# A gated linear attention with an MLP mixer on one core: batch 0's attention laid out by token slot, one load queue, and a new order

## The chip, the cores and the metric

The kernel runs on one core of one Trainium2 chip. The metric is device time in microseconds (us) of one execution. A core has five engines with queues of their own: TensorE (PE, matmuls; its weight loads are shown as PEld), VectorE (DVE), ScalarE (ACT), GpSimd (POOL) and SyncE (SP, which only issues transfers). Each queue is worked off in its order; an instruction at its head that waits holds everything behind it.

## The reference

Two parts follow each other. For each of 4 batches and 8 heads, a 48 x 48 state runs over 768 tokens, and its output goes through a mixer over tokens and then over channels:

```python
for t in range(S):                      # S = 768, per batch and head, D = 48
    state = alpha[:, :, t, :, None] * state + einsum('bhd,bhe->bhde', k[:, :, t], v[:, :, t])
    y[:, :, t] = einsum('bhd,bhde->bhe', q[:, :, t], state)
x  = y as (4, 768, 384)
h  = relu(x.T @ w_tok1) @ w_tok2        # 768 -> 256 -> 768, over tokens
u  = x + h.T
h2 = relu(u @ w_ch1) @ w_ch2            # 384 -> 1536 -> 384, over channels
out = u + h2
```

Inputs and output are float32; the kernel multiplies in bf16.

## The kernel before

**Tiling.** The tokens of a batch are cut into three blocks of 256, so there are 12 blocks n = 3b + k. A partition holds two neighbouring tokens, called slots (0 and 1), so 128 partitions hold a block; partitions 0 to 63 are its first half (128 tokens, hf 0), 64 to 127 its second (hf 1). A load (`ld_at`, `ld_kt`, `ld_qt`, `ld_vt`) brings 384 KB.

**Attention of a block.** `ln` takes the logarithm of alpha, a matmul with a triangular matrix (`cum`, `cumw`) sums it up along a half, and two exponentials give E and IE. `qq` = q x E and `kk` = k x IE (L642). Both are transposed: for blocks below NX = 6 on PE (`trk`, `trq`, L654) with a copy out of PSUM (`evk`, `evq`), for later blocks by a DMA transpose on SP (`dk`, `dq`, L664), where q needs one more copy (`pq`). `G0_`, `G1_` multiply keys with queries on quarter tiles of the array (48 rows by 64 columns); `mask` (L700, DVE only) zeroes what lies in the future. `K` sums k v over each half of a block; from it come the states `s0`, `s1`: for a first half directly (L747), else by `sa` (add the earlier state, L750) and `sm` (multiply by the decay, L753). `ia`, `ib` multiply queries with the earlier state and `y0_`, `y1_` add the masked part; `x` (L684 or L685) copies the result out of PSUM. A block yields two x tiles of 128 tokens.

For `K` and `y` to contract over 128 partitions, the tokens of one half have to lie over all partitions: `vs0`, `vs1` swap halves of v, and `ka`, `kb`, `kc` (L722) turn halves of k. These are copies of 64 partitions.

**Batch 0** (blocks 0 to 2, `WIDE`) keeps both slots apart up to the exponentials (`lnw`, `cumw`, L626), and a short `Et` (L630) takes the totals; later blocks fold the slots first (`P`, `k0a`, `q0r`).

**Mixer of a batch.** `t1` (L787) and `ht`, then `t2` (L792) and `u` (L796), then u is transposed: for batches in `UP` = (0, 1) on PE (`up`, L803, with the copies `ut`), for the others by DMA (`ux`, L668). `c1` (L811, 24 groups of three matmuls) and `rt` (L782 on ACT, L784 on DVE), `c2` (L816, groups of three), `o` (L820) and the store `st` (L574). Weights come as float32 in 16 loads (`ldw_`) and are cast (`cw_`). `t2` of batch 0 needs the six x tiles and the casts of w_tok1 and w_tok2.

**The order.** Nothing is scheduled at run time. `ORDER` names every step with its engine in its last letter (t PE, s ACT, v DVE, g POOL, y SP), and each engine's queue is this list with the others left out. `BUFS` names the buffer of each value; 19 buffers of the class `in` hold all loads and raw weights, and a load waits for the last reader of its buffer. Each DMA also waits for an earlier one whose semaphore it takes over. Steps named `f1_...` and `f3_...` are matmuls on a zero tile `zs` whose result is not used; L593 is the helper `mm` through which they and all small matmuls go, so its line stands for many steps. A semaphore also orders DVE and POOL operations that share their SBUF port (`shared`).

Of the kernel before, what the change touches and what calls it, by code (L numbers as in the profile page):

```python
# [11 lines left out]
ALU = mybir.AluOpType  # L12
# [85 lines left out]
NX = 6  # L98
KFN = 0
LAST = (3, 0)  # L100
UP = (0, 1)
# [9 lines left out]
WIDE = (0, 1, 2)  # L111

# [3 lines left out]
def build(g):  # L116
# [8 lines left out]
    def filler(nm, bank):  # L125
        return [P.op(f"f{z}_{nm}", {"PE": pe([512] * z)["PE"], "NONE": (0.0, 0.0)}, -100, writes=[bank],
                     emit=lambda e, z=z: g.fill(bank, z)) for z in (1, 3)]

    def attention(n):
# [8 lines left out]
        def fill(nm, bank):  # L138
            return filler(f"{nm}{n}", bank) if n < NB else []

        at, kt, qt, vt = V("in"), V("in"), V("in"), V("in")
        ld = {}
        for v, nm in ((at, "at"), (kt, "kt"), (qt, "qt"), (vt, "vt")):
            ld[nm] = P.op(f"ld_{nm}{n}", {"SP": (420.0, 420.0), "ACT": (374.0, 374.0)}, -90000.0 + 10 * n, writes=[v],
                          emit=lambda e, v=v, nm=nm: g.load(e, nm, v, b, k, ld[nm]), dma=("i", IN_NS, 1500.0, 650.0))
        la, E, IE = V("la"), V("E"), V("IE")
        pkk, pkq, vb = V("pkk"), V("pkq"), V("vb")
        k_in, q_in = [ld["kt"]], [ld["qt"]]
        if n in WIDE:
            lnp = O("ln", act(800, True), 0, writes=[la], reads=[at], preds=[ld["at"]], emit=lambda e: g.lnw(la, at))  # L150
            cb = V("pair")
            cum = O("cumw", pe([384] * 4 + [4] * 8 + [16]), 2, writes=[cb, E, IE], reads=[la], preds=[lnp] + fill("cumw", cb),
                    emit=lambda e: g.cumw(cb, la))
            e1 = O("E", act(768), 4, writes=[E], reads=[cb], preds=[cum], emit=lambda e: g.exps(E, cb, 1.0))
            et = O("Et", act(16), 6, writes=[E], reads=[cb], preds=[cum], emit=lambda e: g.exptot(E, cb))
            e2 = O("IE", act(768), 3, writes=[IE], reads=[cb], preds=[cum], emit=lambda e: g.exps(IE, cb, -1.0))
        else:
# [8 lines left out]
            e1 = et = O("E", act(400), 4, writes=[E], reads=[cb], preds=[cum], emit=lambda e: g.expE(E, cb))  # L166
            e2 = O("IE", act(384), 4, writes=[IE], reads=[cb], preds=[cum], emit=lambda e: g.expIE(IE, cb))
# [12 lines left out]
        if n < NX:  # L180
            bk, bq = V("one"), V("one")
            trk = O("trk", pe([128] * 8), 8, writes=[bk], reads=[pkk], preds=[kk] + fill("trk", bk),
                    emit=lambda e: g.trw(bk, pkk))
            evk = O("evk", either(dve(1024, True), act(1024)), 9, writes=[tpk], reads=[bk], preds=[trk],
                    emit=lambda e: g.trwev(e, tpk, bk))
            trq = O("trq", pe([128] * 8), 8, writes=[bq], reads=[pkq], preds=[qq] + fill("trq", bq),
                    emit=lambda e: g.trw(bq, pkq))
            evq = O("evq", either(dve(1024 * 1.065), act(1024 * 1.34)), 9, writes=[tpq], reads=[bq], preds=[trq],
                    emit=lambda e: g.qev(e, tpq, g.bank(bq).bitcast(BF16)))
        else:  # L190
            evk = O("dk", {"SP": (1240.0, 1240.0)}, 9, writes=[tpk], reads=[pkk], preds=[kk],
                    emit=lambda e: g.xbar(tpk, pkk), dma=("x", 1400.0, 1180.0, 480.0))
            tqx = V("tpk")
            xq = O("dq", {"SP": (1240.0, 1240.0)}, 9, writes=[tqx], reads=[pkq], preds=[qq],
                   emit=lambda e: g.xbar(tqx, pkq), dma=("x", 1400.0, 1180.0, 480.0))
            evq = O("pq", either(dve(1024), act(1024 * 1.35, True), {"POOL": (1100.0, 1140.0)}), 9.5, port=True, writes=[tpq], reads=[tqx], preds=[xq],
                    emit=lambda e: g.qev(e, tpq, g.t(tqx)))
        gtm = V("gtm")
        masks = []
        for hf in range(2):  # L200
            gp = V("pair")
            G = O(f"G{hf}_", pe([128] * 4), 10 + hf, writes=[gp], reads=[tpk, tpq], preds=[evk, evq] + fill(f"G{hf}", gp),
                  emit=lambda e, hf=hf, gp=gp: g.gmm(gp, tpk, tpq, hf), mode="G")
            masks.append(O(f"mask{hf}_", dve(1024), 12 + hf, writes=[gtm], reads=[gp], preds=[G],
                           emit=lambda e, hf=hf, gp=gp: g.mask(gtm, gp, hf)))
        nst = 2 if k < NB - 1 else 1
        kp = V("pair")
# [4 lines left out]
        vsw = lambda hf, preds: shift(f"vs{hf}_", 10, [vb], [vt], preds, lambda e: g.vswap(e, vb, vt, hf))  # L212
        turned = n >= KFN
        if turned:
            vs = [vsw(hf, [vc]) for hf in range(2)]
            kx, kp_in = None, [kk, vc, vs[0]]
            if nst == 2:
                kx = V("kt")
                ka = shift("ka", 9, [kx], [pkk], [kk], lambda e: g.kturn(e, kx, pkk, 0))
                kb = shift("kb", 9, [kx], [pkk], [kk], lambda e: g.kturn(e, kx, pkk, 1))  # L220
                kp_in += [ka, kb, vs[1]]
            kc = shift("kc", 9, [pkk], [], [kk, trk if n < NX else evk] + ([ka] if nst == 2 else []),
# [4 lines left out]
        else:  # L227
            KO = O("K", {"PE": (276.0 if nst == 2 else 140.0, 420.0)}, 9.5, writes=[kp], reads=[pkk, vb],
                   preds=[kk, vc] + fill("K", kp) + ([prev_s[1]] if prev_s and k > 0 and n > NB else []),
                   emit=lambda e: g.kmm(kp, pkk, vb, nst), mode="G")  # L230
            vs = [vsw(hf, [KO, vc]) for hf in range(2)]
        before = prev_s if k > 0 else None
        states = [before]
        for hf in range(nst):
            s_, sp = V("ss"), states[-1]
            if sp is None:
                so = O(f"s{hf}_", dve(384), 10, writes=[s_], reads=[kp, E], preds=[KO, et],
                       emit=lambda e, s_=s_, hf=hf: g.sfirst(s_, kp, E, hf, wide, turned))
# [636 lines left out]
```

## Time and profile before

| | us |
|---|---|
| runs | 166.53, 166.59, 167.32 (median 166.59) |
| span of the profiled execution, first to last instruction | 165.0 |
| PE busy | 156.2 (1683 matmuls) |
| DVE busy | 121.2 |
| ACT busy | 96.2 |
| POOL busy | 68.7 |
| the 38 matmuls on `zs`, all before 27 us | 12.7 |
| first `t2_0` matmul (L792) | starts at 32.90 |
| first `c1_0` matmul (L811) | starts at 37.34 |
| end of the last `o` (L820) | 162.42 |

The profile gives the profiled execution's span and no other time of it; the median of the runs is 1.6 us above the span. Busy time counts an instruction from start to end. Matmuls overlap, so a matmul of 326 ns can follow another after 162 ns. What an engine waited for is inferred from semaphores. The granted TensorE clock is 1.00 over the whole execution.

Load data come to 25.17 MB read; the DMA engines are busy in 9 tenths or more of nearly every slice up to half of the span.

### The profile page before, as it was taken

What the parts mean: (1) busy time and instruction counts of PE and PEld (TensorE: products, weight loads), DVE (VectorE), ACT (ScalarE), POOL (GpSimd) and SP (SyncE); (2) the same over time, 40 slices, a digit from 0 to 9 for tenths busy, and PEclk for the clock granted to TensorE, in tenths of its full rate; (3) what the DMA queues carried; (4) which work ended last, traced back from release to release, by engine and by line L of the source; (5) the groups of instructions that cost most, each with busy time, mean ns of one, the idle gap of its engine ahead of it and who ended that gap; (6) DMA issues with size and microseconds to landing.
All of it is one profiled execution on the core that took longest, in us unless ns stands there. A gap on an engine that the chain in (4) does not pass through costs nothing.

```text
span 165.0 us, 4235 instructions
## 1 busy us (share of the span) xinstructions
PE 156.2 (95%) x1683; PEld 99.2 (60%) x1683; DVE 121.2 (73%) x210; ACT 96.2 (58%) x186; POOL 68.7 (42%) x84
## 2 busy tenths in 40 slices
PE   7969769999999999999999999999999999999992
PEld 2435446666666766576666666666666656656662
DVE  4098989989898898798878999989492455524422
ACT  3599987998877837939887746913614001514110
POOL 4025659497217475792388528973300000000000
PEclk9999999999999999999999999999999999999999
DMA  4999999999999999999989996898001136200213
GB/s 121 324 325 325 337 347 316 365 327 352 371 335 347 326 315 226 307 252 264 136 198 255 211 250 120 219 181 183 0 4 48 49 75 157 105 0 0 99 72 119
DMA packets 74531, 34.48 MB, mean 209 GB/s; under 512 B 67984, under 2 KB 73488, under 8 KB 74512
## 3 DMA queue, kind: packets, MB, share of 16 engines
q1 hardware_dynamic: 50576, 23.30, 55.2%
q10 hardware_dynamic: 23936, 10.91, 24.3%
q8 instruction: 13, 0.21, 0.5%
q14 instruction: 6, 0.05, 0.1%
HBM read 25.17 MB, written 4.72 MB: 181 GB/s over the span
## 4 chain that ended last, share of the span: by engine, by line
PE 83%; DMA 4%; SPq 3%; POOL 2%; issue 2%; ACT 2%; DVE 1%; POOLq 0%; DVEq 0%
PE ps L816 29%; PE ps L811 29%; PE ps L593 14%; PE ps L792 5%; DMA in<-in_v_dram 4%; PE ps L787 4%; SPq L534 3%; PE ps L654 1%; PE ps L803 1%; POOL pkk L642 1%; DVE gtm L700 1%; POOL vb L685 1%; ACT x L684 1%; POOL ss L753 1%; ACT E L626 0%
## 5 line engine op out<-in xcount | busy, mean ns | idle before, releaser
L816 PE MATMUL ps<-wc,rt 128*128 128x384 bf16 (+1 forms) x300 | 54.7, 320 | 0.0
L811 PE MATMUL ps<-ut,wc 128*128 128x384 bf16 x288 | 51.3, 326 | 0.0
L782 ACT ACTIVATE rt<-ps 128x384 bf16<-128x384 f32 x54 | 24.4, 490 | 35.4 <-PE ps L811 34.7
L811 PEld LDWEIGHTS <-wc 128*128 128x128 bf16 x288 | 27.1, 98 | 16.7
L816 PEld LDWEIGHTS <-rt 128*128 128x128 bf16 x300 | 27.5, 98 | 15.9
L700 DVE TENSOR_TENSOR gtm<-ps,mk 128x1024 bf16<-128x1024 f32 x24 | 28.7, 1219 | 4.8 <-PE ps L593 3.4
L784 DVE TENSOR_SCALAR rt<-ps 128x384 bf16<-128x384 f32 x42 | 21.7, 551 | 9.2 <-PE ps L811 9.2
L820 DVE TENSOR_TENSOR o<-ps,u 128x384 f32<-128x384 f32 (+1 forms) x25 | 13.1, 537 | 10.0 <-PE ps L816 9.1
L685 POOL CAST vb<-in 64x384 bf16<-64x384 f32 (+1 forms) x18 | 10.9, 608 | 15.2 <-DVE pkk L642 8.9
L593 PE MATMUL ps<-zs 128*128 128x512 bf16 x38 | 12.7, 452 | 2.9 <-DVE zs L496 1.1
L684 ACT CAST x<-ps 128x384 bf16<-128x384 f32 x17 | 7.8, 477 | 10.7 <-PE ps L593 10.5
L796 DVE TENSOR_TENSOR u<-ps,x 128x384 bf16<-128x384 f32 x24 | 11.8, 550 | 3.0 <-PE ps L792 3.0
L642 DVE TENSOR_TENSOR pkq<-in,E 128x768 bf16<-128x768 f32 x8 | 7.6, 954 | 5.4 <-ACT E L626 5.2
L787 PE MATMUL ps<-x,wt 128*128 128x384 bf16 x48 | 11.1, 325 | 0.5 <-DVE gtm L700 0.4
L684 ACT CAST vb<-in 64x384 bf16<-64x384 f32 (+1 forms) x18 | 11.1, 618 | 0.7 <-DMA in<-in_v_dram 0.2
L642 POOL TENSOR_TENSOR pkk<-in,IE 128x768 bf16<-128x768 f32 x5 | 9.1, 1816 | 4.9 <-DVE pkk L685 3.2
L753 POOL TENSOR_TENSOR ss<-tmp,E 128x384 bf16<-128x384 f32 x11 | 9.2, 833 | 3.2 <-DVE tmp L750 2.9
L750 DVE TENSOR_TENSOR tmp<-ps,ss 128x384 f32<-128x384 f32 x16 | 8.8, 552 | 1.0 <-PE ps L593 0.5
L792 PE MATMUL ps<-ht,wt 128*128 128x384 bf16 x48 | 9.5, 326 | 0.0
L593 PEld LDWEIGHTS <-gtm 128*128 128x128 bf16 x192 | 7.4, 96 | 2.7 <-DVE gtm L700 0.9
L593 PEld LDWEIGHTS <-tpk 48*64 48x64 bf16 x384 | 6.1, 106 | 4.9 <-issue 4.3
L593 PE MATMUL ps<-vb,gtm 128*128 128x48 bf16 x192 | 8.6, 183 | 0.4 <-DVE gtm L700 0.4
(91 smaller groups left out, 216.6 us busy)
## 6 DMA issues: line engine op xcount, KB each, us to landing
in<-in_moe_w_ch_dram SPq DMA_DIRECT2D x10, 384.0 KB, 6.2
in<-in_alpha_dram SPq DMA_DIRECT2D x9, 384.0 KB, 6.8
out_dram<-o SPq DMA_DIRECT2D x16, 192.0 KB, 2.5
in<-in_q_dram SPq DMA_DIRECT2D x7, 384.0 KB, 6.3
in<-in_v_dram ACTq DMA_DIRECT2D x7, 384.0 KB, 6.0
in<-in_k_dram ACTq DMA_DIRECT2D x6, 384.0 KB, 5.7
in<-in_k_dram SPq DMA_DIRECT2D x6, 384.0 KB, 6.2
in<-in_v_dram SPq DMA_DIRECT2D x5, 384.0 KB, 7.2
```

The costliest lines, as they stand in the source:

```text
L593: return self.pe.matmul(out, lhsT=lhsT, rhs=rhs, start=start, stop=stop, skip_group_check=True)
L642: self.shared(self.eng[e].tensor_tensor(self.t(dst)[:, :, :, 0:D], self.t(src).rearrange("p h s d -> p s h d"), bass.AP(tensor=f.tensor, o ...
L684: return self.act.copy(d, s)
L685: return self.shared(self.eng[e].tensor_copy(d, s))
L700: self.nc.vector.tensor_tensor(self.t(gtm)[:, hf, :, :], self.pair(gp).rearrange("p a (j t) -> p (a j) t", t=128), bass.AP(tensor=m.tensor ...
L782: self.act.activation(d, s, AF.Relu)
L784: self.nc.vector.tensor_scalar_max(d, s, 0.0)
L787: self.pe.matmul(self.bank(bank)[:, 0:HD], lhsT=self.wt1[:, kc, m * 128 : m * 128 + 128], rhs=self.t(x), start=(kc == 0), stop=(kc == NS - 1))
L792: self.pe.matmul(self.bank(bank)[:, 0:HD], lhsT=self.wt2[:, kc, i * 128 : i * 128 + 128], rhs=self.t(hts[kc]), start=(kc == 0), stop=(kc = ...
L811: self.pe.matmul(self.bank(bank)[:, 0:HD], lhsT=self.wc1[:, kc, mc * 128 : mc * 128 + 128], rhs=self.t(ut)[:, 3 * half : 3 * half + 3, kc, ...
L816: self.pe.matmul(self.bank(bank)[:, 0 : cz - ca], lhsT=self.t(rts[mc][0])[:, i * 128 : i * 128 + 128], rhs=self.wc2[:, mc, ca:cz], start=( ...
L820: self.nc.vector.tensor_tensor(self.t(o)[:, ca:cz], self.bank(bank)[:, 0 : cz - ca], self.t(u)[:, i % 3, ca:cz], ALU.add)
```

## The change

- **Token slots for batch 0.** G, mask, K and y of blocks 0 to 2 get new forms (`gslot`, `maskslot`, `khalf`, `yslot`). G's tile is now all pairs of one slot's keys with the queries of both halves; mask uses a new tile `mkw` (130 columns, shifted by the slot). K and y contract over 64 partitions (one half) and sum over the two slots; half 0 uses rows 0 to 63 of the array and half 1 rows 64 to 127, each with its own PSUM bank. So `vs`, `ka`, `kb`, `kc` drop out for these three blocks. `y` is one step for both halves and needs both masks.
- **States of batch 0.** The earlier state is added in PSUM by a matmul with the identity (`kadd`, steps `A0_`, `A1_`), and one multiplication (`s`, DVE) gives the new state: `sa` and `sm` drop out.
- **Exponentials of batch 0.** Both PSUM banks carry the totals, E is one instruction over 800 columns, and `Et` drops out.
- **Queues.** All loads are issued by SP (`LOADQ`); stores stay on SP or ACT.
- **Transposes.** The keys of block 5 go by DMA (`KX`), its queries stay on PE; u of batch 1 goes by DMA (`UP`). The query transposes themselves, bf16 in PSUM, are as before.
- **Weights.** The first half of w_ch1 is cut into three pieces of 256 columns, each of which serves two `c1` column blocks.
- **Empty matmuls.** They may stand before many more steps, in counts of 1 to 12; the new order has 31 of them: 12 before cumw0, 8 before trq0, then 1, 1, 3, 1, 2 and, before the first t2, 3.
- **Order and buffers.** `ORDER` and `BUFS` are new from the first to the last entry.

The core of the diff:

```diff
-NX = 6
+KX = (5, 6, 7, 8, 9, 10, 11)
+QX = (6, 7, 8, 9, 10, 11)
 KFN = 0
...
-UP = (0, 1)
+UP = (0,)
...
+HALVED = ()
+LOADQ = ({"SP": (420.0, 420.0)}, {"SP": (420.0, 420.0)})
...
-    def filler(nm, bank):
-        return [P.op(f"f{z}_{nm}", {"PE": pe([512] * z)["PE"], "NONE": (0.0, 0.0)}, -100, writes=[bank],
-                     emit=lambda e, z=z: g.fill(bank, z)) for z in (1, 3)]
+    def fillers():
+        for o in list(P.ops):
+            nm = o.name
+            if "PE" in o.eng and (nm[:4] in ("t1_0", "t2_0", "up_0") or nm.split("_")[-1][-1] in "0123" and nm[:2] not in ("t1", "t2", "up", "c1", "c2") and not nm.endswith("10") and not nm.endswith("11")):
+                bank = V("one")
+                for z in (1, 2, 3, 4, 6, 8, 12):
+                    P.op(f"f{z}_{nm}", {"PE": pe([512] * z)["PE"]}, -100, writes=[bank],
+                         emit=lambda e, z=z, bank=bank: g.fill(bank, z))
...
-            ld[nm] = P.op(f"ld_{nm}{n}", {"SP": (420.0, 420.0), "ACT": (374.0, 374.0)}, -90000.0 + 10 * n, writes=[v],
-                          emit=lambda e, v=v, nm=nm: g.load(e, nm, v, b, k, ld[nm]), dma=("i", IN_NS, 1500.0, 650.0))
+            for z, h0, h1 in (parts if nm in ("at", "kt") else whole):
+                key = nm + z
+                ld[key] = P.op(f"ld_{key}{n}", LOADQ[n >= 6], -90000.0 + 10 * n, writes=[v],
...
-            e1 = O("E", act(768), 4, writes=[E], reads=[cb], preds=[cum], emit=lambda e: g.exps(E, cb, 1.0))
-            et = O("Et", act(16), 6, writes=[E], reads=[cb], preds=[cum], emit=lambda e: g.exptot(E, cb))
-            e2 = O("IE", act(768), 3, writes=[IE], reads=[cb], preds=[cum], emit=lambda e: g.exps(IE, cb, -1.0))
...
-        if n < NX:
-            bk, bq = V("one"), V("one")
-            trk = O("trk", pe([128] * 8), 8, writes=[bk], reads=[pkk], preds=[kk] + fill("trk", bk),
-                    emit=lambda e: g.trw(bk, pkk))
-            evk = O("evk", either(dve(1024, True), act(1024)), 9, writes=[tpk], reads=[bk], preds=[trk],
+        if n in KX:
+            evk = O("dk", {"SP": (1240.0, 1240.0)}, 9, writes=[tpk], reads=[pkk], preds=kk,
+                    emit=lambda e: g.xbar(tpk, pkk), dma=("x", 1400.0, 1180.0, 480.0))
+            k_read = evk
...
+            kps = [V("one") for _ in range(nst)]
+            K = O("K", {"PE": (350.0, 530.0)}, 9.5, writes=kps, reads=[pkk, vb], preds=kk + [vc],
+                  emit=lambda e, first=before is None: g.khalf(kps, pkk, vb, first), mode="Y")
+            for hf in range(nst):
+                kp, s_, sp = kps[hf], V("ss"), states[-1]
+                KO = K
+                if sp is not None:
+                    KO = O(f"A{hf}_", pe([384]), 9.6 + hf, writes=[kp], reads=[sp[0]], preds=[K, sp[1]],
+                           emit=lambda e, kp=kp, s0=sp[0]: g.kadd(kp, s0))
+                so = O(f"s{hf}_", dve(384), 10 + hf, writes=[s_], reads=[kp, E], preds=[KO, et],
+                       emit=lambda e, s_=s_, kp=kp, hf=hf: g.sfirst(s_, kp, E, hf, wide))
+                states.append((s_, so))
...
+            yo = O("y", {"PE": (440.0, 580.0)}, 14, writes=yps, reads=[gtm, vb], preds=masks + [vc] + helds[0] + helds[1],
+                   emit=lambda e, st=states[:2]: g.yslot(yps, gtm, vb, [not q for q in st]), mode="Y")
...
-        o = P.op(f"ldw_{nm}{piece}", {"SP": (420.0, 420.0), "ACT": (374.0, 374.0)}, prio, writes=[raw],
+        o = P.op(f"ldw_{nm}{piece}", LOADQ[0], prio, writes=[raw],
...
-                         reads=[ut], preds=(uts[0:2 + half] if b in UP else [uts[half]]) + [wl[("wc1", mc // 6 * 3 + p)] for p in range(3)],
+                         reads=[ut], preds=(uts[0:2 + half] if b in UP else [uts[half]]) + [wl[("wc1", p)] for p in ([mc // 2] if mc < 6 else (3, 4, 5))],
...
-            h, c = divmod(piece, 3)
-            self.gated(dma(t, self.w[2][128 * c : 128 * c + 128, 768 * h : 768 * h + 768]), op)
+            if piece < 3:
+                self.gated(dma(t.rearrange("p (c m) -> p c m", c=3),
+                               self.w[2][:, 256 * piece : 256 * piece + 256].rearrange("(c p) m -> p c m", p=128)), op)
+            else:
+                c = piece - 3
+                self.gated(dma(t, self.w[2][128 * c : 128 * c + 128, 768:1536]), op)
...
+    def expEw(self, E, cb, h0, h1):
+        ca, cz = h0 * D, h1 * D if h1 < H else 400
+        self.act.activation(self.t(E).rearrange("p (s c) -> p s c", s=2)[:, :, ca:cz], self.pair(cb)[:, :, ca:cz], AF.Exp)
...
+    def gslot(self, gp, tpk, tpq, sl):
+        tk, tq = self.t(tpk), self.t(tpq)
+        for j in range(4):
+            for hf in range(2):
+                for r in range(2):
+                    pr = slice(r * 64, r * 64 + D)
+                    self.mm(self.bank(gp, r)[hf * 64 : hf * 64 + 64, j * 128 : j * 128 + 128],
+                            tk[pr, (sl * 4 + j) * 128 + hf * 64 : (sl * 4 + j) * 128 + hf * 64 + 64],
+                            tq[pr, j * 256 + hf * 128 : j * 256 + hf * 128 + 128], True, True)
+
+    def maskslot(self, gtm, gp, sl):
+        m = self.mkw[:, 1 - sl : 129 - sl]
+        self.nc.vector.tensor_tensor(
+            self.t(gtm)[:, sl], self.pair(gp).rearrange("p a (j t) -> p (a j) t", t=128),
+            bass.AP(tensor=m.tensor, offset=m.offset, ap=[list(m.ap[0]), [0, 8], [1, 128]]), ALU.mult)
+
+    def khalf(self, kps, pkk, vb, first):
+        kk, vv = self.t(pkk), self.t(vb)
+        for j in range(4):
+            for sl in range(2):
+                for hf, kp in enumerate(kps):
+                    ph = slice(hf * 64, hf * 64 + 64)
+                    self.mm(self.bank(kp)[:, 96 * j : 96 * j + 96], kk[ph, sl, 2 * j : 2 * j + 2, :],
+                            vv[ph, sl, 2 * j : 2 * j + 2, :], j == 0 and sl == 0, (first and hf == 0) and sl == 1)
+
+    def kadd(self, kp, s0):
+        self.mm(self.bank(kp)[:, 0:HD], self.idn, self.t(s0), False, True)
+
+    def yslot(self, yps, gtm, vb, first):
+        gg, vv = self.t(gtm), self.t(vb)
+        for h in range(H):
+            for sl in range(2):
+                for hf in range(2):
+                    ph = slice(hf * 64, hf * 64 + 64)
+                    self.mm(self.bank(yps[hf])[:, h * D : h * D + D], gg[ph, sl, 4 * (h % 2) + h // 2, :],
+                            vv[ph, sl, h, :], first[hf] and h == 0 and sl == 0, h == H - 1 and sl == 1)
...
 ORDER = """
...
+ld_at1y ld_at0y ln0s ln1s f12_cumw0t cumw0t ld_vt0y vb0g E0s ld_kt0y ld_qt0y ld_at2y ld_qt1y IE0s qq0v kk0v cumw1t
+ld_kt1y E1s qq1v ld_at3y IE1s ld_qt2y ld_vt1y ld_kt2y ld_vt2y f8_trq0t trq0t ln2s ld_at4y kk1v ld_kt3y evq0s ldw_wt10y
+ld_vt3y ld_qt3y f1_trk0t trk0t evk0s ldw_wt11y cumw2t E2s ldw_wt21y ldw_wt20y P3g qq2g ld_kt4y ldw_wc13y IE2s kk2g
+ldw_wc15y ldw_wc14y vb2g ldw_wc11y trq1t ld_at5y K0t s0_0v evq1s G1_0t mask1_0v P4g f1_G0_0t G0_0t mask0_0v ldw_wc12y
+ld_qt4y lnP3s trk1t evk1v A1_0t s1_0v ib0t vb1s ldw_wc10y ld_kt5y f3_y0t y0t x1_0v K1t A0_1t x0_0v cum3t E3s IE3s
+ln13s G1_1t s0_1v k0a3g kk3g f1_ib1t ib1t A1_1t trq2t evq2s trk2t ln14s ia1t mask1_1v lnP4s s1_1v ld_vt4y G0_1t evk2v
+f2_G0_2t G0_2t K2t ia2t A0_2t mask0_1v y1t mask0_2v cw_wt10s t1_0_0_0t x1_1s vb3g kb3g ld_qt5y ldw_wc21y t1_0_1_0t
+vs0_3g G1_2t x0_1s trk3t t1_0_0_1t s0_2v ib2t r14s cum4t mask1_2v y2t ka3s t1_0_1_1t t1_0_1_2t t1_0_0_2t r13s kc3g
+vs1_3s K3t cw_wt11s x0_2v t1_0_1_3t x1_2v t1_0_1_4t t1_0_1_5t q0r3g t1_0_0_3t t1_0_0_4t qq3g s0_3v ht_0_1v ldw_wc20y
+cw_wt21s cw_wt20s IE4s t1_0_0_5t ht_0_0v f3_t2_0_2t t2_0_2t sa1_3v u_0_2v t2_0_3t E4s u_0_3v evk3s k0a4g t2_0_1t
...
```

348 lines of the change are left out of this document (178 added, 170 removed), and 22 rows, old and new, of the table BUFS.

## The prediction

> **What bounds the kernel now.** I read the page's parts 1 and 2 first, then the windows by stage, the chain of waits in order of time, and the groups of instructions with shapes kept apart.
>
> ```profile
> PE 156.2 (95%) x1683; PEld 99.2 (60%) x1683; DVE 121.2 (73%) x210; ACT 96.2 (58%) x186; POOL 68.7 (42%) x84
> ...
> DMA  4999999999999999999989996898001136200213
> ```
>
> TensorE is busy nearly throughout. The stages show where it is not:
>
> ```profile
> 10.00:20.00 10.00, 8.19 (x120) 4.97 (x117) 8.95 (x12) 9.76 (x17) 6.16 (x9) 1.00 1.17 327
> 20.00:30.00 10.00, 7.64 (x151) 5.38 (x151) 9.20 (x13) 8.19 (x15) 6.72 (x8) 1.00 1.07 336
> 30.00:40.00 10.00, 9.92 (x133) 6.82 (x133) 9.07 (x16) 9.19 (x18) 8.32 (x9) 1.00 1.09 350
> 40.00:50.00 10.00, 10.00 (x90) 6.52 (x86) 8.97 (x17) 8.38 (x18) 2.19 (x4) 1.00 1.11 351
> ```
>
> The columns are PE, PEld, DVE, ACT, POOL, then clock, DMA share and GB/s. Before 30 us PE has gaps, and part of what counts as busy is the 38 matmuls on `zs` that compute nothing; DVE (9 of 10) and the DMA engines (full, 327 GB/s) set the pace. From 30 us on PE is full. So there are two prices: up to the first mixer of batch 0 an edit is worth what it moves the chain; behind it, an edit is worth the PE work it adds or removes, as long as nothing is late for PE. I take the first `t2_0` matmul (L792), at 32.90 us in the timeline, as the border. The chain has these pieces of both sorts:
>
> ```profile
> 14.06 7.23 DMA in<-in_v_dram
> ...
> 23.31 1.83 POOL pkk L642
> ...
> 32.99 2.06 PE ps L792 x12
> ...
> 41.16 0.45 PE ps L654 x8
> ...
> 50.71 0.35 PE ps L593 x16
> 51.06 0.59 PE ps L811 x3
> ...
> 109.04 7.31 PE ps L811 x45
> ...
> 162.06 0.36 DVE o L820
> ```
>
> A 384-column matmul takes 7.31/45 = 0.162 us in the flow, a group of three 0.49; a 128-column transpose 0.45/8 = 0.056. The span is 165.0 us; the median of the runs is 166.59, so I count 1.6 us around the span and make the sum on 166.6.
>
> **Part 1, the start: the load order.** For every early load I added the DMA view's time to landing to its issue. The landings, in order, are at 5.0, 5.6, 7.6, 8.3, 9.1, 10.3, 11.5, 12.8, 14.0, 15.1, 17.8, 19.1, 20.5, 21.3, 22.8, 23.7, 24.8, 25.8, 27.6, 28.6, 29.6 and 30.6 us: some 1.2 us a place, with the DMA engines full and, from 2 to 14 us, nearly all of it from the SP queue alone. So I take the places as given, also for one queue, and let the change fill them in its own order: qt1 7th, kt1 8th, vt1 11th, kt2 12th, vt2 13th, wt10 16th, the last of wt2 21st. kt2 comes 1 us earlier than now (13th), vt2 3 us earlier (16th, 23.7). The new SP queue waits at its 7th load for `ln0` (5.0 + 0.84) and at the 8th to 12th for readers on POOL and DVE, but five loads are then still in flight at 1.2 us each, so the engines do not run dry.
>
> **Part 2, the start: the chain to t2_0.** Durations by shape:
>
> ```profile
> L700 DVE TENSOR_TENSOR gtm<-ps,mk 128x1024 bf16<-128x1024 f32 x24 | 28.7, 1219 | 4.8 <-PE ps L593 3.4 <-ACT lf L590 1.0
> ...
> L642 DVE TENSOR_TENSOR pkk<-in,IE 128x768 bf16<-128x768 f32 x7 | 6.7, 954 | 1.1 <-POOL vb L685 0.6 <-issue 0.3
> ...
> L685 DVE CAST x<-ps 128x384 bf16<-128x384 f32 x7 | 3.8, 549 | 0.4 <-PE ps L593 0.4
> ...
> L685 DVE COPY tpk<-ps 128x1024 bf16<-128x1024 bf16 x4 | 2.6, 683 | 0.0
> ...
> L747 DVE TENSOR_TENSOR ss<-ps,E 128x384 bf16<-128x384 f32 x4 | 2.2, 548 | 0.0
> ```
>
> In the changed order DVE does, from kk1 to the second ht: kk1, six masks, two evk, five s of batch 0 and s0_3, six operations of this size on x and ht (four x, two ht). That is 0.95 + 6 x 1.22 + 2 x 0.68 + 6 x 0.55 + 6 x 0.55 = 16.2 us. kk1 cannot start before kt1 (12.8), so DVE alone ends at 29.0. I followed its waits: s0_0 waits for K0 (PE at 13.4) little; mask1_0 for evk0, which on ACT stands behind IE1, ln2 and evq0 (13.9), +0.15; x1_0 to s0_1 for K1, whose vb1 needs vt1 (17.8 + 0.84), +0.2; mask0_2 for evq2 (22.7), +0.1; x0_2 for y2, 0.7 behind mask1_2; in sum about 1.1. ht ends at 30.2. ACT casts the last piece of wt2 from 29.6 to 30.45, so t2_0 starts at 30.5 instead of 32.9: **-2.4**. Bounds: 29.5 (DVE dense) and 32.0 (two more waits of an eviction's length, 0.7 each).
>
> What makes this chain short is what batch 0 no longer does: the 13 half-partition moves vs, ka, kb, kc (about 0.5 us each on ACT and POOL), three Et (0.18 on ACT), and the pair sa + sm (0.56 + 0.83 on POOL or 0.56 on DVE), which becomes one s on DVE plus a 0.16 matmul A on PE. On PE that is four A, 0.65 us, and eight matmuls for K2 in place of four (+0.17), all before t2_0 where PE has gaps. The `vs` that mask and y waited for is gone. The 24 load issues of some 0.38 us on ACT's queue go to SP.
>
> The new 64-row groups (three K, three y) are costed like the groups they replace, 0.34 and 0.4 us, since the G groups on quarter tiles run 16 matmuls in 0.35 us. That row shows another cost: the L811 group behind G takes 0.59 instead of 0.49. Six new groups change the tile shape twice each, 12 x 0.1 = 1.2 us at most; they lie where PE waits, so I count 0 (without that cover the sum would be 1.2 higher, 165.2). TensorEngine Tiling, Key Properties, of the Trainium skill says that a change of tiling mode drains the engine, which speaks against this change; the trace agrees, with the 0.10 us.
>
> **Part 3, behind t2_0.** PE loses up_1 (18 transposes, 1.0) and trk5 (8, 0.45); trq3 now stands behind t2_0 (+0.45): **-1.0**. The six u adds and two ut copies in front of the first c1 are 8 x 0.55 = 4.4 us, and PE has 0.45 more to do meanwhile; 5.05 us from t2_0 to c1 instead of 4.5, of which 0.45 is counted: **+0.2** with the rounding.
>
> Batch 1's u goes through two DMA transposes. The later u transposes landed 3.2 to 3.9 us after issue, the tpk ones, among loads, 3.0 to 6.8. Between the third u add and the first c1_1 PE has eight c2 groups, three cum and three t2 less the adds' lag, 3.9 + 0.8 + 1.0 - 1.0 = 4.7 us; the second half has 4.1. So 0 to 2.7 us of wait; nearest the shorter row, as few loads are then queued: **+0.3**.
>
> dk5 stands on SP behind 36 loads, and vt5 and the last three wc2 pieces behind dk5. It waits for kk5, last of a packed POOL row: kk2 from 19.1, then vb2, P4, k0a3, kk3, vb3, moves, q0r3, qq3, k0a4, kk4 end at 33.5; three casts, sm1_3, P5, ka4; qq4 waits for q0r4 on DVE (40.7); k0a5, kc4, kk5 end at 45.8. The loads ahead end at place 36, 47.4, so the queue does not run dry. dk5 lands at 48.9 to 52.7; G0_5 comes up on PE, by counting its groups from c1 at 35.5, at 52.8. wc24 lands at 54.1 to 56.5, its consumer c2_0_2_2 comes at 58.3. Cost 0, with margins near 0 and 1 us.
>
> The tail: o_3_3 now ends 0.5 us in front of the last half row, and its 192 KB store lands in 2.2 to 2.5 us where the 96 KB one takes 1.6: **+0.3** (bounds 0 and 0.6).
>
> Sum: 166.6 - 2.4 - 1.0 + 0.2 + 0.3 + 0.3 = **164.0**. Its own range: 29.5 for 30.5 and no transpose wait give 162.7; 32.0 gives 165.5.
>
> **Rivals.**
>
> SP held by dk5 (slower). One in-order queue replaces two. If kk5 is late, everything behind dk5 is late: PE first waits for G0_5 at once, from about 46 us on, then for wc24 from a dk5 issue of 48.3, and a us of delay is a us of span. For: POOL is packed, 8.32 of 10 busy between 30 and 40 us already now, and its 1.82 us multiplications are in front; SP waited 6.6 us for one POOL result at a transpose in the present trace. Against: vb2, P4 and the casts have slack. It decides from 3.4 us late; at 5 us the time is 164.0 + 5 = 169.0, at 4 us 168.0.
>
> The start is hidden anyway. wt20 stays 21st; if its cast on ACT, behind a 1.31 evq2, ln14, lnP4, two x and three casts, or the places themselves slip by 1.5, t2_0 starts near 32.2: 165.7.
>
> The change does not do what it says: the 64-row pairs do not overlap. K is then 0.68 and y 0.8 us; K0 and y2 on the chain add 0.34 + 0.4: 164.8.
>
> The clock. With 31 instead of 38 empty matmuls PE could fall to the slow state of its first fills (0.43 us each until 6.4 us, 0.21 after). The longest hole I find in the new order is 1.3 us, before K1; the present trace has 1.5 (the longest wait of PEld) at full clock (PEclk 9 in all 40 slices). If it fell once at 18 us, PE's 6 us of groups to t2_0 would double and some 3 would show: 167.0. TensorE: Matmul & The Clock Gate, Part 1, of the Trainium skill puts the idle window after which the clock halves at about 3.4 us; by it this rival falls away, and no run here shows such a window.
>
> **How the numbers follow.** Forecast 0.56, SP 0.20, hidden 0.13, no overlap 0.08, clock 0.03. What can be told from no change is 0.5%, 165.8 to 167.4. Faster: 0.56 + 0.08 + about 0.05 of "hidden" = 0.69; same: 0.08 + 0.02 of the clock = 0.10; slower: the rest, 0.21. Low end 162.0, below the own range by the tail and part 3 at their best; high end 167.6, which leaves out most of the SP rival and nothing else. The likeliest case alone: 162.7 to 165.5.
>
> **What would show it.** The first L871 matmul (t2) at 30.5, with kt2 and vt2 landed by 20.5; DVE full between 13 and 30; no half-partition copies before 24 us; PE at 10.00 of 10 in every window from 35 us; G0_5 and c1_1 with no PE wait in front; PE's end at 159.1. Wrong would be: PE gaps in front of G0_5, c2_0 or c1_1 (then SP's waits for POOL name the place), t2_0 at 32 or later, or a second stretch of slow clock.

## The result, and the profile after

The changed kernel takes 174.37 us (median of four runs, 171.66 to 175.51), the kernel before beside it 166.60 (166.53 to 167.32): 1.0363 times as long, 95% interval [1.029, 1.0437]. This ratio and those below count only the runs within 1.5% of a kernel's fastest (here 171.66 and 173.86), so they can lie below the quotient of the medians. The forecast was 164.0, with a range of 162.0 to 167.6. The profiled execution has a span of 172.1 us and took 173.86.

The busy times, the slices and the queues on the page of the changed kernel:

```profile
PE 156.0 (91%) x1725; PEld 97.9 (57%) x1725; DVE 110.6 (64%) x199; ACT 93.8 (55%) x175; POOL 79.4 (46%) x87
...
PEclk9999999999999999987999999999999999999999
DMA  5999999999979983898999999999851215010333
```

TensorE does no more work than before (156.2) and DVE 10.6 us less, yet the span is 7.1 us longer. The DMA engines, formerly full up to half of the span and then fading, now have gaps in the first half and are full between 70 and 120 us. The stages (PE, PEld, DVE, ACT, POOL, clock, DMA share, GB/s):

```profile
60.00:70.00 10.00, 10.00 (x89) 6.30 (x87) 4.88 (x10) 4.74 (x11) 6.22 (x6) 1.00 0.59 155
70.00:80.00 10.00, 7.26 (x40) 3.87 (x39) 6.44 (x12) 3.68 (x8) 3.76 (x3) 0.83 1.06 239
...
110.00:120.00 10.00, 9.57 (x73) 5.53 (x62) 8.41 (x14) 5.52 (x13) 4.98 (x5) 1.00 1.11 240
120.00:130.00 10.00, 8.51 (x142) 5.72 (x142) 7.10 (x12) 5.89 (x11) 5.73 (x6) 1.00 0.66 131
```

Before, PE was full in all of these, and from 60 to 70 us the DMA engines moved 276 GB/s instead of 155:

```profile
60.00:70.00 10.00, 10.00 (x128) 6.55 (x126) 8.49 (x14) 7.78 (x17) 6.57 (x7) 1.00 1.16 276
70.00:80.00 10.00, 10.00 (x90) 6.63 (x89) 9.28 (x19) 6.83 (x18) 4.95 (x7) 1.00 1.30 235
...
120.00:130.00 10.00, 10.00 (x93) 6.47 (x91) 5.69 (x9) 2.21 (x5) 0.00 (x0) 1.00 0.06 21
```

Summed over the 10 us windows, 22.1 MB had been moved by 70 us before the change and 18.6 after: the worth of nine loads behind. The last load is issued at 119.45 instead of 100.81.

| | before | after | forecast |
|---|---|---|---|
| first t2_0 matmul | 32.90 | 33.06 | 30.5 |
| from there to PE's end | 129.06 | 135.74 | 128.56 |
| PE's end to the span's end | 3.00 | 3.34 | 3.3 |
| PE waits over 0.25 us behind t2_0, in sum | 0 | 5.69 | 0.3 |

The forecasts of the second and third rows are the steps of the prediction added to the numbers before (129.06 - 1.0 + 0.2 + 0.3; 3.0 + 0.3). So 2.6 us were missed at the start and 7.2 behind it. The largest hole, in the timeline (start, duration, engine, line; in brackets the idle time and what ended it):

```profile
67.98 0.61 SPq L581 DMA_DIRECT2D in<-in_v_dram  x1
69.01 0.97 ACTq L627 DMA_DIRECT2D out_dram<-o  x2
...
73.81 0.56 DVE L743 CAST vb<-in 128x768 bf16<-128x768 f32 x1 [1.34 <-DMA out_dram<-o]
75.96 0.56 DVE L899 TENSOR_TENSOR o<-ps,u 128x384 f32<-128x384 f32 x1 [1.59 <-DMA out_dram<-o]
...
76.57 1.76 PE L890 MATMUL ps<-ut,wc 128*128 128x384 bf16 x5 [2.74 <-DVE o L899]
```

This is one in-order chain. vt6, issued at 67.98 (before: 52.56), lands at 73.7, and only then can DVE cast vb6. The next o needs one of three output buffers, and a store issued at 69.47 lands 6.4 us later, among loads. c1 waits for what DVE does behind that. From 104 us on the chain of waits runs through transposes:

```profile
104.18 5.26 DMA tpk<-pkk
...
110.62 5.79 DMA tpk<-pkq
...
116.97 4.56 DMA tpk<-pkk
```

Before the change no transpose was on the chain.

### The profile page after: what moved, and what is told of

Its sections match the earlier page's. It is cut to its first block, busy times and chain, and to the rows that moved or that the text cites. A ratio compares the mean times of both kernels' runs of the same rounds, so it can differ in the third digit from the quotient of the medians.

```text
span 172.1 us, 4301 instructions
## 1 busy us (share of the span) xinstructions
PE 156.0 (91%) x1725; PEld 97.9 (57%) x1725; DVE 110.6 (64%) x199; ACT 93.8 (55%) x175; POOL 79.4 (46%) x87
## 4 chain that ended last, share of the span: by engine, by line
PE 56%; DMA 22%; DVE 6%; POOL 5%; SPq 5%; issue 3%; ACT 1%; POOLq 0%; DVEq 0%
PE ps L895 22%; PE ps L890 19%; PE ps L646 7%; DMA tpk<-pkk 6%; DMA in<-in_moe_w_tok_dram 4%; DMA out_dram<-o 4%; DMA tpk<-pkq 3%; PE ps L866 3%; PE ps L871 3%; DMA in<-in_k_dram 3%; SPq L581 3%; DMA in<-in_alpha_dram 2%; POOL pkk L700 2%; SPq L597 2%; DVE gtm L758 1%
## 5 line engine op out<-in xcount | busy, mean ns | idle before, releaser
L890 PEld LDWEIGHTS <-wc 128*128 128x128 bf16 x288 | 27.9, 99 | 22.1 <-issue 5.6
L758 DVE TENSOR_TENSOR gtm<-ps,mk 128x1024 bf16<-128x1024 f32 x18 | 21.4, 1219 | 5.1 <-PE ps L646 5.0
L700 POOL TENSOR_TENSOR pkk<-in,IE 128x768 bf16<-128x768 f32 x9 | 16.3, 1815 | 6.5 <-ACT IE L679 2.2
L700 POOL TENSOR_TENSOR pkq<-in,E 128x768 bf16<-128x768 f32 x8 | 14.5, 1813 | 10.0 <-DVE vb L743 3.5
L631 POOL TENSOR_TENSOR in<-in 128x384 f32<-128x384 f32 x8 | 7.9, 998 | 14.1 <-DMA in<-in_alpha_dram 6.7
L742 ACT CAST vb<-in 64x384 bf16<-64x384 f32 (+1 forms) x15 | 9.2, 616 | 6.1 <-DMA in<-in_v_dram 4.0
L646 PE MATMUL ps<-rt 128*128 128x512 bf16 x31 | 9.8, 448 | 1.1 <-DVE rt L538 1.1
L646 PE MATMUL ps<-tpq,tpk 48*64 48x128 bf16 x384 | 8.3, 220 | 2.1 <-DMA tpk<-pkk 2.1
L743 POOL CAST vb<-in 128x768 bf16<-128x768 f32 (+1 forms) x12 | 7.9, 662 | 4.9 <-DMA in<-in_v_dram 3.9
L829 DVE TENSOR_TENSOR tmp<-ps,ss 128x384 f32<-128x384 f32 x12 | 6.7, 556 | 3.0 <-PE ps L646 2.1
L692 POOL TENSOR_TENSOR in<-in,in 128x384 f32<-128x384 f32 x7 | 7.0, 996 | 2.8 <-DMA in<-in_k_dram 1.4
```

Of the source, the lines that this page charges most:

```text
L646: return self.pe.matmul(out, lhsT=lhsT, rhs=rhs, start=start, stop=stop, skip_group_check=True)
L700: self.shared(self.eng[e].tensor_tensor(self.t(dst)[:, :, h0:h1, 0:D], self.t(src)[:, h0:h1].rearrange("p h s d -> p s h d"), bass.AP(tens ...
L742: return self.act.copy(d, s)
L758: self.nc.vector.tensor_tensor(self.t(gtm)[:, hf, :, :], self.pair(gp).rearrange("p a (j t) -> p (a j) t", t=128), bass.AP(tensor=m.tensor ...
L890: self.pe.matmul(self.bank(bank)[:, 0:HD], lhsT=self.wc1[:, kc, mc * 128 : mc * 128 + 128], rhs=self.t(ut)[:, 3 * half : 3 * half + 3, kc, ...
```

## The experiments

All times are medians beside runs of the kernel before on the same chip (166.7 to 167.7). "Holes" are PE waits over 0.25 us behind the first t2_0, summed from the trace. The changed kernel: 5.69.

**Queue, place, or place of the work? (e1 to e4, e8)**

e1, the loads behind dk5 on ACT:

```diff
-ld_vt5y ldw_wc25y ... ld_vt11y
+ld_vt5s ldw_wc25s ... ld_vt11s
```

> The changed kernel, with the 26 loads that its order lists behind dk5 issued by ACT instead of SP. Theory Q (one queue): in the changed kernel SP stood 3.3 us at dk5 and 6.1 us at ux_1_0 with loads behind them that waited for nothing else, the DMA engines ran at 65 and 13 to 28 GB/s at 48 to 50 and 64 to 68 us, and the loads came so late that they crowd with stores and transposes from 68 us on. Then both holes in the DMA rate go, the 2.7 us hole of PE at 74 us goes, PE's windows from 50 to 130 us come to 9.8 or more, and the time falls from 174 to 167 to 169 (the start keeps its loss). Theory T (the added DMA transposes are themselves too slow): PE keeps its holes in front of c1_1 and G, 172 to 175. Theory S (stores that land late block DVE through its three o buffers, whatever the loads do): the hole at 74 us stays, 172 to 175.

190.04, ratio 1.1382 [1.1299, 1.1465]. In the changed `BUFS` a load's buffer is often free only late; on ACT that wait holds ACT's own work (vt6 is issued at 76.6).

e2, three loads in front of the first u transpose:

```diff
-st_0_3s ux_1_0y ld_vt6y ln17s ld_qt7y
+st_0_3s ld_vt6y ld_qt7y ld_kt7y ux_1_0y ln17s
```

> The changed kernel, with three loads (vt6, qt7, kt7) moved in front of the transpose ux_1_0 on the same SP queue; no queue, transpose or buffer changes. Theory Q: the three loads land before 68 us instead of 73.7 to 77.3, vb6 does not hold DVE at 73.8, stores issued near 69 us land in under 4 us instead of 5 to 7, the 2.7 us hole of PE before c1_1 and the slow clock behind it go: 3 to 5 us off, 169 to 171. Theory T: no change, 173 to 175, and PE still waits before c1_1. Theory S: no change, since the stores stand behind the same transpose.

175.82, 1.0473 [1.0389, 1.0556]. vt6 was still issued only at 65.90: its buffer had held at6, whose last reader ln16 ends at 65.8. And now PE waits 3.56 us for ut, which lands 6.8 us after its issue.

e3, u of batch 1 on PE, and e8, the keys of block 5 on PE:

```diff
-UP = (0,)
+UP = (0, 1)
...
-KX = (5, 6, 7, 8, 9, 10, 11)
+KX = (6, 7, 8, 9, 10, 11)
```

> The changed kernel, with the transposes of batch 1's u back on PE (18 matmuls, three copies out of PSUM on DVE and ACT) in place of the two DMA transposes. PE gets 1.0 us of work more. Theory Q: SP no longer stands at ux_1_0, so the loads run on as in the experiment that moves them: 169 to 172. Theory T: the same or better, 168 to 171, with the gain in front of c1_1. It does not tell Q from T by itself: if moving the loads gains as much as taking the transposes out, Q holds; if only this one gains, T.

174.68, 1.0445 [1.0379, 1.051].

> The keys of block 5 back on PE (trk5 in front of trq5, copy evk5 on DVE), so SP is not held from 44 to 48.5. The prediction's rival (SP held by dk5): vt5 to at6 are issued 4 to 5 us earlier, the holes behind shrink by as much: 169 to 171.5. Theory B: kt6 still waits for its buffer until 57 and ux_1_0 for u until 66, so the later loads do not move; PE has 0.45 more: 173.5 to 175.5.

175.63, 1.0513 [1.0448, 1.0577]. So neither DMA transpose is the cause by itself. The forecast's rival (SP held by dk5) falls too: without dk5, vt5 goes out 1.3 us earlier (48.55), but at6 no earlier than in the changed kernel (53.38 and 53.31).

e4, wt10 and wt11 issued by ACT at 13.4 and 17.6 us:

```diff
-ldw_wt10y ... ldw_wt11y
+evq1s ldw_wt10s ... vb1s ldw_wt11s
```

> The changed kernel, with the loads wt10 and wt11 alone issued by ACT, earlier in the order (behind evq1 and behind vb1). The first t2 started at 33.1 us instead of the predicted 30.5, and its last wait was for wt20, landed at 32.2 instead of 29.6. Theory A (one queue cannot bridge its own issue stalls: an issue of 2.4 us at 15.4 left the DMA engines at 216 to 236 GB/s between 18 and 22 us): with a second queue the rate there goes back to 320 or more, wt10 lands by 23, wt20 by 30.5, and t2 starts at 30.5 to 31.5: 1.5 to 2.5 us off the time, unless a later wait takes it. Theory B (the engines of the start, not the weights, set t2): t2 stays within 0.5 us of 33.1.

174.37, 1.0394 [1.0326, 1.0462]. The rate rises (325 against 301 GB/s from 10 to 20 us), but at4 and kt3 come later, PE stands at half clock from 28.76 to 32.17, and t2_0 starts at 34.62. Inconclusive for the start.

**Buffers and earlier loads (e5 to e7, e9, e10)**

In the changed `BUFS`, 11 of the 19 `in` buffers hold nothing from 55 us on, while the other eight are refilled at once. e5 spreads the loads over all of them; e10 also moves three loads, e6 eight, e7 most; e9 is e6 with batch 1's u on PE. The first pair of lines names buffers that `BUFS` gives as bare numbers.

```diff
-kt6: in 2, vt6: in 6, kt7: in 15
+kt6: in 1, vt6: in 16, kt7: in 17
...
-ld_qt6y ... ux_1_0y ld_vt6y ld_qt7y ld_kt7y
+ld_qt6y ld_vt6y ld_qt7y ld_kt7y ... ux_1_0y
```

> ORDER as in the changed kernel; only the `in` buffers of the 28 loads behind dk5 are assigned anew, each the one that has been free longest (in the changed kernel 11 of the 19 `in` buffers stay empty from 55 us on, and 8 are reused at once). Theory B (loads come late, by buffer reuse and by what stands in front of them on SP): kt6 no longer waits 3.5 us and qt6 is issued by 56, but vt6, qt7, kt7 still stand behind ux_1_0 (66.5), so the PE hole at 70-77 stays in part: 172 to 174.5. Theory P (the compute engines' own order is late, the loads are not the cause): 174.4, nothing moves.

173.43, 1.029 [1.0227, 1.0352].

> As e5, and six loads (vt6, qt7, kt7, kt8, vt7, qt8) moved in front of ux_1_0 on SP, two more (vt8, at9) in front of dk6. Theory B: vt6 issued by 60 and landed by 67 instead of 73.7, no cast waits for it, the stores land in under 4 us, PE is busy 9.3 or more in 70-80 at a clock of 0.95 or more; of the 7.8 us lost behind t2_0 some 3 to 5 come back: 169 to 171.5. Theory P: 173.5 to 175.5, the same PE holes behind other releasers. Theory R (a transpose lands late behind loads in one queue): ux_1_0 takes over 5 us to land and PE waits for ut; 173 to 176.

174.05, 1.0401 [1.0336, 1.0466]. vt6 lands at 65.2 as expected, the o hole is gone, and ux_1_0, held behind six loads until 71.1, makes a larger one:

```profile
75.09 2.10 PE L890 MATMUL ps<-ut,wc 128*128 128x384 bf16 x6 [4.44 <-DMA ut<-u]
```

> As e6, and the loads of blocks 8 to 11 spread between the transposes of blocks 6 to 8, the last one right behind dq8 (changed kernel: last load at 119.5). Theory B: the DMA transposes of 104 to 121 land in about 3.5 us instead of 4.6 to 5.8, PE is full there too: 167 to 170. Theory P: 173.5 to 175.5. Theory R: dk7 to dq8 land later than now (over 6.7 us) and PE waits for them in 78-95: 173 to 177.

175.42, 1.0519 [1.045, 1.0587]; the same hole, 4.52.

> As e6 (buffers spread, loads in front), and batch 1's u transposed on PE as before the change. In e6 the one hole left behind t2_0 over 0.5 us is 4.44 us in front of the first c1_1 that reads ut, with the clock at 0.83 behind it (1.7 us more). Theory C (three late transfers hide behind each other, late loads, late stores, late u transposes; each repair alone only uncovers the next): both gone, 18 transposes more on PE: span 171.0 - 4.4 - 1.4 + 1.0 = 166.2, time 167 to 169. Theory P (the compute engines' order is late in itself): the hole comes back behind a cast or a copy, 172.5 to 175.

171.29, 1.0261 [1.0222, 1.03]; holes 4.66, in other places: 1.90 behind DMA transposes, the rest behind ACT, DVE and POOL.

> Buffers spread, only vt6, qt7, kt7 in front of ux_1_0, u of batch 1 by DMA. Theory C with a place for the transposes: ux_1_0 is issued at 66.5 with few loads ahead and lands by 70, ux_1_1 by 76; the hole in front of c1_1 is 0.5 to 1.5 us and the clock stays above 0.95: 168 to 171. Theory R (any load near the transposes delays them): hole 2.5 to 4.5 again, 172.5 to 175.

Four runs between 167.76 and 174.22 (median 171.69), too far apart for a ratio. In the profile the hole at 70 to 80 us is gone, others remain from 84 us on (4.40 in sum):

```profile
70.00:80.00 10.00, 10.00 (x98) 6.14 (x96) 7.85 (x15) 8.59 (x20) 5.86 (x4) 1.00 1.00 199
80.00:90.00 10.00, 8.50 (x98) 5.40 (x95) 7.57 (x13) 6.09 (x12) 3.87 (x5) 1.00 1.19 218
```

The holes move as theory C says, from one late transfer to the next, but its times were missed (e9: 171.29 against 167 to 169). Buffers alone (e5) and places alone (e2) gave nothing that can be told from the changed kernel's own spread. Both together gave nothing either where u stands behind the loads (e6, e7); e9 is lower (170.65 to 171.72), and e10 is too, by its median, though its runs overlap with the changed kernel's.

**One part alone on the kernel before (e11, e12)**

```diff
-ld_at1s ... ld_kt0s ... ld_kt2s ... ldw_wc25s
+ld_at1y ... ld_kt0y ... ld_kt2y ... ldw_wc25y
```

> The kernel before with its 24 load issues of ACT's queue given to SP, at the same places of the order; nothing else. The prediction's step (landing places hold for one queue too): landings within 0.5 us of those of before, t2_0 at 32.9, 166 to 168. Echo theory (with one queue a pause of 2.5 us in the transfers comes back as a pause some 6 us later, because so many loads are in flight and no other queue fills it): landings slip by 1.5 to 3 us from the 15th place on, t2_0 at 34 to 36, and later loads wait in line behind SP's transposes: 169 to 174.

169.87, 1.0151 [1.0076, 1.0225]: one queue alone costs about this much, in an order made for two. In the profiled execution, the slowest of the four (171.08), the place behind t2_0 is one late weight (wc25, issued at 54.9 instead of 50.3):

```profile
61.63 0.83 ACT L684 CAST wc<-in 128x768 bf16<-128x768 f32 x1 [5.47 <-DMA in<-in_moe_w_ch_dram]
62.52 0.48 PE L816 MATMUL ps<-wc,rt 128*128 128x384 bf16 x2 [2.36 <-ACT wc L684]
```

e12 puts the token slots into the order of before:

```diff
-vs1_0g ... ka0s vs0_0g ... kb0s ... Et1s ... kc0g ... sa1_0v ... sm1_0g ... y0_0t ... y1_0t
+A1_0t ... s1_0v ... y0t
```

> The kernel before with only batch 0's attention by token slot put into its order: vs, ka, kb, kc, Et of blocks 0 to 2 dropped, sa and sm replaced by A (PE) and s (DVE) at their places, one y per block, weights of w_ch1 cut as in the changed kernel; loads on two queues, transposes and everything else as before. Prediction, part 2 (less work off PE makes the start shorter): t2_0 at 31 to 32, 164.5 to 166. Rival (the start is bound by the last piece of w_tok2, which lands at 29.6 as before, and by the DVE queue): t2_0 at 32.5 to 33.5, 166 to 167.5.

171.84, 1.0268 [1.0205, 1.0331]. Behind t2_0 only 0.77 us of holes, but t2_0 starts at 38.03, with PE at half clock from 25.84 to 29.26 and from 32.67 to 36.08. That is not all of it: the one run with a mean clock of 1.00 still took 170.43. In an order not made for it the new attention is a loss; which of its waits is to blame was not separated.

**Loads on ACT with free buffers (e13 to e15)**

```diff
-dk5y ld_vt5y ... ld_vt11y
+ld_vt5s ... dk5y ... ld_vt11s
...
-st_1_1y ... st_1_3y
+st_1_1s ... st_1_3s
```

> Buffers spread as in e5, and the 28 loads behind dk5 issued by ACT, spread over ACT's queue at one load per 1.2 us from 46 us on (1.7 behind the 19th), so that none waits for a buffer; SP keeps the transposes and its stores. Theory Q (the one SP queue is what costs behind 43 us: loads wait behind transposes, transposes land late behind loads): no wait of SP for a transposition input holds a load, dk5 lands by 52, vt6 by 63, DMA transposes land in 2.7 to 4 us, holes behind t2_0 under 2.5 us in sum: 165.5 to 168.5. Theory D (total DMA traffic is what delays, whichever queue): transposes still land in 4.5 us and more, 170 to 174.

186.21, 1.112 [1.1012, 1.1228].

> As e13, and the stores st_1_1 and st_1_3 on ACT instead of SP, where they stand in front of dk10 and dq11. If the stores on SP delay these transposes (e10: 1.19 in front of c1_2 and 0.70 in front of G_11, SP held 1.2 us for o): 0.5 to 1 us less than e13. If they only wait where SP waits anyway for POOL: the same as e13 within 0.5.

186.08, 1.1119 [1.1068, 1.1171]: the stores change nothing. The timeline of e13 shows where it is slow: the issues themselves hold ACT. The first four take 0.37 to 0.43 us, later ones up to 3.66; PE is left idle and stands at half clock from 80.30 to 97.36. That the issues are long because more loads are queued than the DMA engines move is likely, but not shown.

```profile
51.78 3.12 ACTq L581 DMA_DIRECT2D in<-in_k_dram  x1
54.93 1.30 ACT L742 COPY tpq<-ps 128x1024 bf16<-128x1024 bf16 x1 [1.92 <-issue]
```

> As e10, with eight of the loads behind ux_1_1 issued by ACT at places where they wait for no buffer, some 2 us or more apart (vt7, vt8, at9, kt9, at10, kt10, vt10, vt11), and qt8 moved in front of dk7 on SP. In e10 SP issues without a pause from 71 to 100, dk7 and dk8 land 6 to 6.7 us after issue, at9 lands at 89.8 and PE waits 0.77 for its logarithm and 1.11 for the state behind it. Theory Q with pace (one queue costs, and ACT can carry loads as long as they are fewer than the engines move): these two holes go, dk7 and dk8 land in under 5 us, the holes behind t2_0 fall from 4.4 to under 3: 166.5 to 169.5. Theory D (traffic in sum, not the queue): dk7 and dk8 land as late as in e10, 170 to 173.

176.24, 1.0423 [1.0334, 1.0513]. ACT is not held now (its issues take 0.40 to 0.62 us), but dk7, issued with three loads in flight, lands 9.7 us later, and PE waits 3.21 us for what stands behind it. Theory Q falls in the form that it was given, theory D (the traffic, not the queue) is left; that one queue costs nothing is not shown (e11).

**The traffic taken away (e16, e17)**

17 of the 24 loads of batches 2 and 3 bring one head of eight; the other heads are computed from what the buffers hold. e17 does the same to the kernel before.

```diff
     def load(self, e, nm, v, b, k, h0, h1, op):
+        if b >= 2 and nm != "at" and (b, k, nm) != (3, 2, "vt"):
+            h1 = 1
         src = self.src[nm][b, h0:h1, k * 256 : (k + 1) * 256, :]
```

> The changed kernel, order and buffers as they are, but 17 of the 24 loads of batches 2 and 3 (k, q and v; not alpha, not vt11) bring one head of eight, 48 KB instead of 384, so some 5.7 MB less are moved and the other heads are computed from what lies in the buffers; every instruction on the engines stays. Theory L (late transfers make the loss behind t2_0: the loads and what lands late behind them): holes behind t2_0 under 2 us in sum against 5.7, no clock fall, 165.5 to 169. Theory P (the engines' queues are late in themselves, the wait for a transfer only names the last in line): holes of 4 us and more stay, 172 to 175.

167.35, 1.0009 [0.9969, 1.0049].

> The same 17 loads cut to one head in the kernel before. It has no hole behind t2_0 and its late loads land 4.6 us (median) ahead of their first reader, so less traffic should give nothing: 166 to 167.5 by every theory. If it came out faster by more than 1 us, the traffic would slow PE in another way than by waits.

167.43, 1.0003 [0.9971, 1.0035]. With the same order, buffers and queues and every engine instruction, the loss is gone; the control does not move. The windows of e16:

```profile
70.00:80.00 10.00, 9.21 (x60) 5.35 (x57) 7.63 (x16) 7.75 (x17) 6.07 (x6) 1.00 0.92 198
...
110.00:120.00 10.00, 10.00 (x124) 6.55 (x122) 9.06 (x17) 6.86 (x15) 4.65 (x4) 1.00 0.73 165
```

From t2_0 to PE's end it takes 129.80 (the changed kernel 135.74, e17 129.04), of which 1.69 are holes, and the clock behind t2_0 stays at 1.00. Theory L is shown: late transfers make the loss behind t2_0, not the engines' queues. How much of their lateness comes from the one queue, from the order and from the buffers is not separated.

## Why the prediction was wrong

**What bounds the kernel: the step that failed.** "From 30 us on PE is full", and behind t2_0 an edit is worth its PE work "as long as nothing is late for PE". The condition was examined for three transfers (dk5, u of batch 1, wc24) and taken as given for the 24 loads and the transposes of batches 2 and 3, though the new order moves all of them. Their lead can be read from the traces, as the time from a load's landing to the start of its first reader, for loads that land after 52 us:

| | before | after | e10 | e16 |
|---|---|---|---|---|
| loads | 25 | 28 | 28 | 28 |
| median lead, us | 4.64 | 1.09 | 1.43 | 2.51 |
| with less than 1 us | 1 | 12 | 9 | 8 |
| dk9, dk10, dk11: landing to the first G, us | 7.9, 5.8, 5.4 | 0.0, 0.0, 0.8 | 0.0, 0.0, 1.1 | 1.8, 0.9, 0.8 |

The transfers did not get slower as such: keys' transposes take 5.3 us (median) before and 4.6 after. Before, the order issued them 8.7 us or more ahead of the G groups of blocks 9 to 11; now it is 4.2 to 5.3. The 7.2 us are 5.69 of holes, 0.3 of them forecast, and 1.7 of half clock behind the largest one (last section).

**The start.** "So I take the places as given, also for one queue." The 5th to the 14th landing came within 0.4 us of the list; the 15th to the 21st came 1.1 to 2.6 late, since the rate had fallen, as the windows of the changed kernel show (last column GB/s):

```profile
18.00:19.00 1.00, 0.23 (x12) 0.23 (x13) 0.67 (x2) 0.71 (x1) 0.00 (x0) 1.00 0.63 141
19.00:20.00 1.00, 1.00 (x37) 0.77 (x30) 0.41 (x1) 0.14 (x1) 0.91 (x1) 1.00 1.04 291
20.00:21.00 1.00, 1.00 (x27) 0.73 (x17) 0.92 (x2) 1.00 (x3) 1.00 (x2) 1.00 0.77 195
```

Before, the same three microseconds had 325, 355 and 351:

```profile
18.00:19.00 1.00, 0.65 (x10) 0.49 (x10) 0.89 (x3) 1.00 (x3) 0.92 (x2) 1.00 1.17 325
```

From 18 to 22 us the difference is 454 KB, 1.2 loads. Both kernels have an SP issue of 2.4 us at 15.3; before, ACT's loads (kt2, wt10) went on beside it. e11, with one queue, has the same dip (155, 247, 261). wt20 landed at 32.15 instead of 29.6, and t1 waited for the casts:

```profile
25.85 0.50 PE L866 MATMUL ps<-x,wt 128*128 128x384 bf16 x2 [1.32 <-ACT wt L742]
...
31.11 1.15 PE L866 MATMUL ps<-x,wt 128*128 128x384 bf16 x6 [1.31 <-ACT wt L742]
```

The order up to t2_0 is the same in 14 profiles, this one among them. In all of them the rate from 18 to 22 us is below the 340 GB/s of before (195 to 272) and wt20 lands later (29.97 to 32.22); t2_0 begins between 30.92 and 33.66, median 32.26. So 1.8 us of the miss are the rule, and the rest is the luck of this execution. The earliest is 0.4 from the forecast, so nothing here speaks against the sum for the DVE chain, but it was not tested by itself. The rival "the start is hidden anyway" (32.2) named the mechanism and the size.

**PE work, -1.0: right.** Without the holes e16 takes 128.11 from t2_0 to the end of PE, before 129.06: -0.95.

**t2_0 to c1, +0.2:** 4.53 us instead of 4.44, so +0.1.

**u of batch 1 by DMA, +0.3 (0 to 2.7):** under-sized. In the changed kernel no PE wait over 0.25 us ends with a transpose of u, since c1 waits longer for o; in other orders with loads around it the hole reached 4.44 (e6), with little traffic 0.79 (e16).

**dk5, 0:** right for PE, wrong on the way. dk5 was issued at 48.45 instead of 45.8, and the queue did run dry (65 GB/s from 48 to 50 us), but G0_5 had 3.1 us to spare. The point from which it decides, 3.4 us late, was not reached, and e8 shows that undoing it gives nothing.

**64-row pairs:** they overlap. The two matmuls of a pair start 3 to 5 ns apart, and a K of 16 takes 0.51 us, no more than the K of block 2, which has only 8; that rival falls. **The tail, +0.3:** right (3.34 for 3.00).

**The clock** did fall here, behind t2_0 and not at 18 us, as a consequence of the hole (last section). But the rival's chance was set too low: in 8 of the 14 profiles with this start PE fell to half clock once before t2_0, from 19.36 us (e9) at the earliest to 28.20 (e8) at the latest, though no hole of over 3.4 us precedes it. Its price was too high: the median start of t2_0 is 32.27 in these eight and 31.88 in the other six. (The slow fills in the kernel before end at 5.8 us, not at 6.4.)

## What to carry over

A full engine stays full only while the transfers run ahead of it: when an order is remade, compare the lead of every transfer (landing to first reader) and the MB moved by a given time with the old trace, above all in the stages that look safe. Look for buffers that stay empty while loads wait. Whether late transfers are the cause shows in one run that cuts the bytes and leaves the instructions.

## What the hardware showed

**Half clock behind a step of 3.41 us that is about half idle or more.** After the hole of 2.74 us (clock in the column before the DMA share):

```profile
76.00:77.00 1.00, 0.43 (x2) 0.25 (x2) 1.00 (x3) 0.00 (x0) 1.00 (x2) 0.66 0.57 56
77.00:78.00 1.00, 1.00 (x5) 0.44 (x3) 1.00 (x3) 0.00 (x0) 0.28 (x1) 0.50 1.17 260
78.00:79.00 1.00, 1.00 (x5) 0.44 (x3) 0.90 (x3) 0.32 (x1) 0.00 (x0) 0.50 1.07 242
79.00:80.00 1.00, 1.00 (x5) 0.50 (x4) 0.90 (x1) 0.53 (x2) 0.00 (x0) 0.63 0.82 182
```

It is back after 3.41 us, so some 1.7 us of work are lost. In all 19 traces the stretches of half clock begin and end on a grid of steps of 3.41 us that runs on through the execution. It goes by how much of a step PE was idle, not by the length of one hole. In the step ahead of 76.32 here PE was busy for 0.92 us, in e11 ahead of 63.01 for 1.05, in e16 ahead of 19.61 for 1.66, with no hole over 1.6 us: half clock followed each. The hole of 2.04 in e5 was cut by the end of a step (busy 2.03 us in the first, 2.76 in the second), and the clock stayed at 1.00. Of the steps at full clock in all traces, those idle for more than 0.6 of their length were all followed by half clock (21 of 21), those idle for less than 0.4 never (828); in between it was 12 of 28. TensorE: Matmul & The Clock Gate, Part 1, of the Trainium skill speaks of an idle window of about 3.4 us and of as long a busy one; both lengths agree with these rows, but a window half idle could be enough.

**A DMA transpose lands by the traffic in flight.** Over 217 transposes of keys and queries in the 17 profiles with full loads, the median from issue to landing is 3.1 us with no load in flight, 4.2 with one, 4.7 with two and 6.7 with three or more; single ones differ widely (2.8 to 10.6 with two). The queue of the loads makes no visible difference for the better: with three in flight, all on ACT's queue, the median is 7.1 (10 transposes), all on SP's own 6.4 (7). In e15 three of the five loads around dk7 were on the other queue, and it still took 9.7 us: DMA: Bandwidth & Descriptors, Issuing engines are not separate DMA queues, of the Trainium skill says that transfers of all issuers run on the same 16 engines and interleave, and the trace agrees. It adds that another issuer saves only the time of the issue, which is usually small beside the transfer; here an issue held ACT for up to 3.66 us (e13).

**Open:** how the lateness is shared between the queue, the order and the buffers; why one issue takes 2.4 us at 15.3 in both kernels; why runs of e10 differ by 6.5 us; and whether an order with the old lead, on one queue, would reach 164.
